# An attention-and-gated-MLP kernel with K and V of one head laid over all 128 partitions, some transposes moved to the DMA crossbar, and a new order list

## The chip, the cores and the metric

The kernel runs on one core of one Trainium2 chip. The metric is the device time of one execution in microseconds, the median of several runs. The engines are TensorE (PE, with its weight loads as PEld), VectorE (DVE), ScalarE (ACT), GpSimd (POOL) and SyncE (SP, which here only issues transfers).

## The reference

```python
def phi(x):                                        # x: [8, 8, 576, 64]
    proj = np.einsum('bhsd,df->bhsf', x, w_phi)    # 64 -> 128 features
    proj = proj - np.max(np.abs(proj), axis=-1, keepdims=True)
    return np.concatenate([np.exp(proj), np.exp(-proj)], axis=-1)
q_p, k_p = (phi(q), phi(k))
kv = np.einsum('bhsf,bhsd->bhfd', k_p, v)
z = np.sum(k_p, axis=2)
num = np.einsum('bhsf,bhfd->bhsd', q_p, kv)
den = np.einsum('bhsf,bhf->bhs', q_p, z)[..., None] + 1e-06
x = num / den                                      # then heads side by side: [8, 576, 512]
gate = sigmoid(sum over 5 taps k of conv_w[k] * x shifted down by 4 - k)
out = (gate * (x @ w_val)) @ w_out
```

There are 8 batches of 8 heads with 576 tokens of 64 numbers each. All inputs and the output are float32; the kernel multiplies in bf16.

## The kernel before, in words

**Tiling.** Two heads make a unit: `hp` is the pair, so units 0 to 31 are four per batch. A head's 576 tokens are 64 rows of 9 (`J`); token 9p + j lies on partition p in "plane" j. One head of the pair uses partitions 0 to 63, the other 64 to 127. Planes 0 to 7 of a unit are its main part; plane 8 of all four units of a batch is a "tail" unit (32 to 39).

**Steps of a unit**, each a function `op_...` and a token of the order list:

- `LD`: GpSimd issues the load of K, Q or V of a batch (of one or two units in batch 0), with the cast to bf16 in the transfer (L311). Each of K, Q, V has three buffers.
- `T` (L329, tails L325): TensorE transposes K and Q, eight 128x128 products into one PSUM bank; `C` copies the bank to the tile `T` in SBUF (L197 on VectorE or L195 on ScalarE). There are five such tiles.
- `PK`, `PA` (L341): projections of K and Q with tokens on partitions, into two banks each, as products on half the array's rows (64 of 128), in pairs. `MK`, `MQ` (L359): VectorE takes the maxima of absolute values.
- `K0`, `K1` (L384): ScalarE's two exponentials of K's projection, into `KT`. `E` (L378): exp of minus and plus the maximum, two small instructions per unit. `V` (L409, L413): GpSimd multiplies V by that, into `VT`, with a column for the sum z.
- `KV` (L427): TensorE sums KT x VT over the tokens, 36 half-array products per unit, the two heads in two banks; `KM` copies them to `KVSA`.
- `PQ` (L441): Q's projection with features on partitions; `SH` (L450): eight products subtract the maximum in PSUM; `X0`, `X1` (L384): the exponentials into `QT`.
- `N` (L492, tails L481): numerator and denominator; `XN` (L510, L512): reciprocal and product; `XP` transposes XN into `XT`, by the DMA crossbar from SP's queue (L531) for 28 units, on TensorE with a copy `XX` for the others.

**Steps of a batch.** `HL` copies the halo of four planes in `XT` (L197). `GF` (L571): the five conv taps as 80 products on 32x32 pieces of the array; `TH` (L595): tanh. `VA`, `VB` (L600): x @ w_val; `GV` (L616): gate. `OA`, `OB` (L629): @ w_out; `OE` (L638, L640): copy to SBUF; `ST`, `SL` (L650): store. `GT` (L673), `VT` (L684), `HT`, `GW`, `OT`, `OF`, `SU` do the same for plane 8, with 64x64 pieces for the taps.

**What sets the order.** Each engine takes its instructions strictly in the order of the string `ORDER`, a list of tokens: `PK.5@0,1` is the step PK of unit 5 into PSUM banks 0 and 1, `:D`, `:A`, `:P` name VectorE, ScalarE or GpSimd. PSUM has eight banks, all given out by the list. An instruction that waits holds up everything behind it on its engine, and the transfers behind it on its queue.

Of the kernel before, what the change touches and what calls it, by code (L numbers as in the profile page):

```python
# [20 lines left out]
HP = 4  # L21
J = 9
E1 = D + 1

# [3 lines left out]
LW.0 LC.0 CK.0:D LD.0 CQ.0:A LD.1 LD.2 LD.3 W.0:A LD.4 T.0@6 C.0:D LD.5 ND.0:D PK.0@4,5 PA.0@6,7 LD.6 K0.0  # L28
MQ.0 LD.7 K1.0 T.1@3 LD.8 PQ.0@0,1 MK.0 C.1:A SH.0 LD.9 X0.0 PK.1@2,3 PA.1@6,7 LD.10 MK.1 E.0 X1.0 V.0:P MQ.1
K1.1 TP.0@1 T.2@5 E.1 PQ.1@6,7 C.2:D K0.1 SH.1 LD.11 CW.0:D PK.2@4,5 X1.1 T.32@0 MK.2 LD.12 PA.2@2,3 X0.1  # L30
C.32:D MQ.2 E.2 K0.2 PK.32@6,7 LD.13 V.1:P MK.32 K1.2 PQ.2@2,3 T.3@0 SH.2 E.32 C.3:D K0.32 V.32:P X1.2
PA.3@0,1 MQ.32 PK.3@4,5 MQ.3 V.2:P K1.32 X0.2 PQ.32@6,7 SH.32 MK.3 KV.1@0,1 X0.32 KV.0@2,3 X1.32 DG.0:P KM.1:D
K1.3 N.1@6,7 PQ.3@0,1 K0.3 XN.1 SH.3 KM.0:D LW.1 XP.1 T.33@6 X1.3 N.0@2,3 C.33:D PK.33@6,7 X0.3 XN.0 KV.2@4,5
MK.33 T.4@1 MQ.33 E.33 T.5@0 KM.2:A C.4:D K0.33 N.2@2,3 K1.33 C.5:D T.6@1 E.3 T.7@5 XN.2 C.6:A V.3:P PK.4@6,7
C.7:D XP.2 PA.5@2,3 K1.4 MQ.5 PA.4@4,5 XP.0 PK.5@0,1 K0.4 CV.0:P MQ.4 PQ.5@2,3 SH.5 K1.5 MK.4 KV.3@4,5 X0.5
KM.3:D X1.5 PQ.4@6,7 MK.5 SH.4 E.4 X1.4 N.32@2 T.34@3 XN.32 N.3@4,5 C.34:D E.5 V.4:P X0.4 T.10@3 XN.3 XP.32@2
C.10:D XX.32:A PA.6@6,7 XP.3 PK.6@4,5 K0.5 MQ.6 T.9@3 V.33:P T.8@2 K0.6 C.9:D PQ.6@6,7 V.5:P K1.6 KV.4@0,1
C.8:D SH.6 KM.4:D MK.6 N.4@0,1 X1.6 LD.14 KV.5@2,3 X0.6 HL.0:D XN.4 GT.0@4,5 LD.15 KM.5:A VT.0 HT.0 E.6
N.5@0,1 V.6:P GF.0@2,3,6,7 XN.5 GW.0 XP.5 VA.0@0 TH.1 XP.4 VB.0 LD.16 PK.7@4,5 TH.0 KV.6@6,7 MK.7 CO.0:P
VA.3@1 KM.6:A VB.3 GV.0 K0.7 VA.1@7 GV.3 N.6@2,3 E.7 VA.2@6 K1.7 XN.6 VB.1 VB.2 XP.6 GV.1 PK.34@0,1 PA.7@2,3  # L40
GV.2 V.7:P K0.34 PQ.33@4,5 SH.33 MQ.7 OA.1@7 K1.34 OA.0@6 X0.33 OB.0 X1.33 MK.34 PQ.7@2,3 LD.17 PK.8@4,5 MQ.34
E.34 SH.7 OE.0:A MK.8 V.34:P KV.7@0,1 X0.7 OB.1 KM.7:D E.8 OA.2@6 X1.7 OE.1:D V.8:P PA.8@0,1 N.33@7 MQ.8 K0.8
N.7@2,3 OB.2 K1.8 XN.7 PQ.8@0,1 SH.8 XN.33 XP.7 PK.9@2,3 OE.2:D X0.8 XP.33@5 OA.3@7 XX.33:D MK.9 OB.3 X1.8
PA.9@4,5 T.11@6 OE.3:A MQ.9 KV.8@0,1 K0.9 T.35@7 KM.8:D E.9 PQ.9@4,5 C.35:D K1.9 SH.9 V.9:P C.11:D N.8@0,1
HL.1:D X1.9 PK.10@6,7 XN.8 GT.1@2,3 VT.1 MK.10 HT.1 X0.9 LD.18 KV.9@0,1 GW.1 KM.9:A LD.19 PA.10@4,5 K1.10
N.9@2,3 MQ.10 OT.0@0 K0.10 XN.9 PQ.10@4,5 E.10 SH.10 OF.0:D V.10:P XP.9 GF.1@2,3,6,7 X0.10 XP.8 X1.10 ST.1
VA.4@1 VA.7@0 TH.3 PK.11@4,5 VB.4 ST.0 MK.11 TH.2 VB.7 KV.10@6,7 GV.7 SU.0 VA.6@3 KM.10:A GV.4 K0.11 VB.6
N.10@6,7 GV.6 K1.11 VA.5@2 XN.10 VB.5 E.11 PK.35@0,1 GV.5 XP.10 PA.11@4,5 V.11:P K0.35 PQ.34@6,7 SH.34 MQ.11
T.12@3 K1.35 OA.4@2 X0.34 OB.4 MK.35 X1.34 PQ.11@4,5 C.12:A OE.4:D SH.11 MQ.35 KV.11@6,7 E.35 X1.11 V.35:P
PK.12@2,3 KM.11:D OA.5@1 MK.12 X0.11 OB.5 LD.20 PA.12@6,7 OE.5:A T.13@0 MQ.12 E.12 N.11@4,5 K1.12 V.12:P  # L50
# [53 lines left out]
def kernel(  # L104
# [24 lines left out]
    featq = pool("featq", 4)  # L129
    featt = pool("featt", 2)  # L130
    vtp = pool("vtp", 4)
    vttp = pool("vttp", 2)
    xnp = pool("xnp", 4)
    mlpp = pool("mlpp", 2)
    outp = pool("outp", 2)
# [15 lines left out]
    def main_tile(name, b):  # L151
        if (name, b) not in main:
            main[name, b] = loadp[name].tile([P, HP, J, D], BF16, name=name + "N")
# [611 lines left out]
```

## Time and profile before

| | |
|---|---|
| runs | 236.83, 240.39, 240.66 us; median 240.39 |
| profiled execution, from first to last instruction | 240.9 us |
| mean granted TensorE clock | 0.979 |
| instructions on PE, DVE, ACT, POOL | 4473, 285, 316, 141 |
| DMA traffic | 30.39 MB in 32982 packets |
| HBM | 30.48 MB read, 9.44 MB written |

The profile takes one execution. A row of its groups reads: line, engine, operation, output <- inputs, shapes, count, then total busy time in us and mean ns of one, then the idle time just before them and what ended it. A matmul's busy time holds its latency, so the distance from start to start in the timeline tells more than the mean. A stage's row gives the stretch and, for each engine, its busy time and number of instructions.

### The profile page before, as it was taken

Reading aid. Unit: us, or ns where it says so; the run is one execution under the profiler, and the core shown is the slowest. Engines: PE = TensorE matmul, PEld = TensorE weight load, DVE = VectorE, ACT = ScalarE, POOL = GpSimd, SP = SyncE. Lnnn points to the kernel's source line nnn. Section 1 sums busy time; section 2 is a strip of 40 time slices with the busy share of each in tenths; the row PEclk is TensorE's granted clock in tenths of the full one; section 3 lists DMA queues with packets and bytes.
Section 4 is the critical chain, followed back from the end, with each engine's and each line's share of the span. In section 5 each row is a group of like instructions: output and inputs, shape, how many; then the busy total and the mean of one; then the engine's idle time right before and its main releaser. Section 6 shows DMA issues by size and latency. Waiting matters only on the chain.

```text
span 240.9 us, 10034 instructions
## 1 busy us (share of the span) xinstructions
PE 208.8 (87%) x4473; PEld 140.6 (58%) x4500; DVE 180.9 (75%) x285; ACT 188.9 (78%) x316; POOL 109.3 (45%) x141
## 2 busy tenths in 40 slices
PE   1777997996998999679998999899995999999990
PEld 1455775853575566556665566666773666676540
DVE  2568599965999699479985899789985588897540
ACT  3688789963997999749988889999994799986531
POOL 8487939774525169135334335333543035542000
PEclk9999999997999999999999999999999799999997
DMA  6999972399936949993969693321559216000476
GB/s 147 280 257 217 209 115 47 41 187 109 143 35 104 249 135 164 201 194 104 179 131 123 94 150 69 69 71 25 112 101 218 88 26 112 3 3 3 129 225 177
DMA packets 32982, 30.39 MB, mean 126 GB/s; under 512 B 16677, under 2 KB 28837, under 8 KB 32938
## 3 DMA queue, kind: packets, MB, share of 16 engines
q0 software_dynamic: 12512, 13.86, 38.1%
q1 hardware_dynamic: 19882, 15.03, 29.5%
q10 hardware_dynamic: 544, 0.85, 1.2%
q8 instruction: 35, 0.57, 1.0%
q14 instruction: 9, 0.07, 0.1%
HBM read 30.48 MB, written 9.44 MB: 166 GB/s over the span
## 4 chain that ended last, share of the span: by engine, by line
PE 60%; DVE 21%; issue 6%; DMA 5%; ACT 5%; POOL 0%; ACTq 0%; DVEq 0%; POOLq 0%
PE PS L600 12%; PE PS L629 9%; PE PS L450 7%; PE PS L427 6%; PE PS L341 5%; PE PS L492 5%; DVE MQA L359 5%; DVE MKA L359 5%; PE PS L571 4%; PE PS L441 4%; PE PS L329 3%; DMA qN<-in_q_dram 3%; DVE T L197 3%; DVE XN L512 3%; ACT QT L384 2%
## 5 line engine op out<-in xcount | busy, mean ns | idle before, releaser
L409 POOL TENSOR_TENSOR VT<-vN,EA 128x1024 bf16<-128x1024 bf16 x32 | 60.9, 1904 | 90.4 <-issue 68.8
L384 ACT ACTIVATE QT<-PS 128x1024 bf16<-128x1024 f32 x64 | 63.2, 1028 | 12.5 <-PE PS L450 12.2
L384 ACT ACTIVATE KT<-PS 128x1024 bf16<-128x1024 f32 x64 | 63.1, 1027 | 2.2 <-DVE MKA L359 1.2
L359 DVE TENSOR_REDUCE MKA<-PS 128x8 f32<-128x1024 f32 (+1 forms) x40 | 44.3, 1112 | 16.3 <-PE PS L341 16.0
L359 DVE TENSOR_REDUCE MQA<-PS 128x8 bf16<-128x1024 f32 (+1 forms) x40 | 44.4, 1112 | 4.5 <-PE PS L341 4.2
L600 PE MATMUL PS<-XT,WVAL 128*128 128x512 bf16 x128 | 33.6, 389 | 2.0 <-issue 1.9
L629 PE MATMUL PS<-WOUT,GV 128*128 128x512 bf16 x105 | 30.4, 382 | 2.1 <-issue 1.6
L341 PE MATMUL PS<-W,T 64*128 64x128 bf16 x512 | 26.6, 232 | 1.9 <-DVE T L197 1.2
L450 PE MATMUL PS<-nident,MQA 128*128 128x128 bf16 x288 | 25.6, 235 | 1.5 <-issue 1.5
L427 PE MATMUL PS<-VT,KT 64*128 64x65 bf16 x1024 | 24.3, 196 | 2.6 <-issue 1.7
L616 DVE SCALAR_TENSOR_TENSOR GV<-GATE,PS 128x512 bf16<-128x512 bf16 x32 | 21.4, 683 | 5.7 <-PE PS L600 4.8
L427 PEld LDWEIGHTS <-KT 64*128 64x128 bf16 x1024 | 20.7, 98 | 6.7 <-issue 3.8
L450 PEld LDWEIGHTS <-MQA 128*128 128x128 bf16 x288 | 18.3, 105 | 10.1 <-issue 9.5
L341 PEld LDWEIGHTS <-T 64*128 64x128 bf16 x512 | 17.0, 100 | 11.5 <-issue 7.2
L512 DVE TENSOR_TENSOR XN<-PS,RCPA 128x512 bf16<-128x512 f32 x32 | 22.1, 691 | 1.1
L492 PE MATMUL PS<-KVSA,QT 128*128 128x65 bf16 x512 | 21.9, 196 | 1.0 <-DVE KVSA L197 0.5
L492 PEld LDWEIGHTS <-QT 128*128 128x128 bf16 x512 | 19.6, 99 | 5.5 <-DVE GVt L699 0.5
L197 DVE COPY T<-PS 128x1024 bf16<-128x1024 bf16 x27 | 18.0, 682 | 3.1 <-PE PS L329 3.0
L595 ACT ACTIVATE GATE<-PS 128x1024 bf16<-128x1024 f32 x16 | 16.0, 1028 | 5.4 <-PE PS L571 5.4
L600 PEld LDWEIGHTS <-WVAL 128*128 128x128 bf16 x128 | 10.9, 99 | 12.7 <-issue 4.0
L329 PE MATMUL PS<-ident_bf,kN 128*128 128x128 bf16 x128 | 13.3, 230 | 5.5 <-DVE kN L197 5.1
L441 PE MATMUL PS<-T,W 64*128 64x512 bf16 x64 | 13.5, 416 | 1.5 <-DVE MQA L359 1.0
(78 smaller groups left out, 293.8 us busy)
## 6 DMA issues: line engine op xcount, KB each, us to landing
out_dram<-OS SPq DMA_DIRECT2D x28, 256.0 KB, 4.2
kN<-in_k_dram POOLq DMA_DIRECT2D x7, 576.0 KB, 6.8
qN<-in_q_dram POOLq DMA_DIRECT2D x7, 576.0 KB, 9.8
vN<-in_v_dram POOLq DMA_DIRECT2D x7, 576.0 KB, 8.7
OS<-in_moe_w_val_dram SPq DMA_DIRECT2D x1, 1024.0 KB, 10.5
out_dram<-OSt SPq DMA_DIRECT2D x8, 128.0 KB, 2.4
OS<-in_moe_w_out_dram SPq DMA_DIRECT2D x8, 64.0 KB, 9.7
out_dram<-OS ACTq DMA_DIRECT2D x4, 128.0 KB, 2.7
```

The lines of the kernel that those rows point to most:

```text
L197: read(engines[eng].tensor_copy(dst, x), bank)
L341: nc.tensor.matmul(PS[:, bank[par], c0 + blk * P:c0 + (blk + 1) * P], u.T[r, i, blk, :], W2[r, :], start=True, stop=True,)
L359: read(nc.vector.tensor_reduce(dst[:, :, 0:n], banks(*bank)[:, :, c0:c0 + n * F].rearrange("p a (b f) -> p a b f", f=F), AX.X, ALU.max, ap ...
L384: read(nc.scalar.activation(dst, banks(*bank)[:, :, 0:n * P].rearrange("p r (x t) -> p r x t", t=dst.shape[-1]), AF.Exp, scale=1.0 if ft = ...
L409: e.tensor_tensor(u.VT[:, :, :, 0:D], x.unsqueeze(1).to_broadcast([P, 2, n, D]), w.unsqueeze(3).to_broadcast([P, 2, n, D]), ALU.mult,)
L427: nc.tensor.matmul(PS[:, bank[h2], ft * E1:(ft + 1) * E1], kt, vt, start=(j == 0), stop=(j == 8),)
L441: nc.tensor.matmul(PS[:, bank[par], 0:n], W2[r, :], u.T[r, 1, :, :].rearrange("p b t -> p (b t)"), start=True, stop=True,)
L450: nc.tensor.matmul(PS[:, u.PQ[par], blk * P:(blk + 1) * P], MQA[:, i, par, blk:blk + 1].to_broadcast([P, P]), nident[:, :], start=False, s ...
L492: nc.tensor.matmul(PS[:, bank[c // 2], x * E1:(x + 1) * E1], u.QT[:, ft, c, h2, :, :].rearrange("p j t -> p (j t)"), kv[:, h2, ft * E1:(ft ...
L512: read(nc.vector.tensor_tensor(u.XN[:, :, :, :], nv[:, :, :, 0:D], rc.unsqueeze(3).to_broadcast([P, 2, 4, D]), ALU.mult,), u.N)
L600: nc.tensor.matmul(PS[:, m.val[jt], :], WVAL[:, dt, jt * P:(jt + 1) * P], planes(xt(m.b), slice(0, P), dt, 4), start=(dt == 0), stop=(dt = ...
L629: nc.tensor.matmul(PS[:, bank, :], lhs(jt), WOUT[:, jt, :], start=(jt == 0), stop=(jt == 3))
```

## The change

- **One head on 128 partitions.** K and V of a head are split in two halves of its rows' planes: partitions 0 to 63 hold planes 0 to 4, partitions 64 to 127 planes 4 to 8 of the same head (`J + 1` planes a unit, plane 4 twice). Each load of K or V becomes two transfers, one for each half. Q stays as it was.
- **KV sums on the whole array.** The two halves of a head are summed in one product on 128 rows: 16 products of 65 columns per unit and 2 of 130 columns for the tail, all in one bank instead of two. The tail's V goes to a zero-padded tile `VTZ` in two parts of 64 partitions. `KVSA` has 16 places instead of 32.
- **Plane-8 taps on the whole array** (`GT`): 20 products with a 128x128 matrix `DIAGF` instead of 40 with 64x64 pieces.
- **Wide projections.** A token with `:W` projects with the zero-padded `W2Z` on the whole array: 4 units and 5 tails of PQ, 8 of PK and PA.
- **Split shifts.** `SH` becomes `SA` and `SB`, each half of the shift; with `:F` the step SA does the whole as before and SB nothing. In the list every SA has `:F`.
- **Crossbar.** `TK` and `TQ` transpose K and Q of units 16 to 31 by DMA from SP's queue, straight into the tile `T`; these units have no `T`, no `C` and no bank for them.
- **E for two units** in one pair of instructions.
- **Fillers.** 24 tokens `FL`: a product of zeros, 512 columns; 12 of them stand behind the last real product.
- **A new list**, with other banks, engines and places for most steps.

Core of the diff:

```diff
-            main[name, b] = loadp[name].tile([P, HP, J, D], BF16, name=name + "N")
+            main[name, b] = loadp[name].tile([P, HP, J if name == "q" else J + 1, D], BF16, name=name + "N")
...
+    def main_dma(eng, name, b, h0, h1, dst):
+        x = src[name][b, 2 * h0:2 * h1, :, :]
+        if name == "q":
+            eng.dma_start(
+                dst.rearrange("p a j d -> p a (j d)"), x.rearrange("(hp t) (p j) d -> (t p) hp (j d)", t=2, j=J),
+            )
+            return
+        x = x.rearrange("h (p j) d -> p h (j d)", j=J)
+        for r in range(2):
+            eng.dma_start(
+                dst[r * 64:(r + 1) * 64, :, :, :].rearrange("p a (t j) d -> p (a t) (j d)", t=2),
+                x[:, :, r * 4 * D:(r * 4 + 5) * D],
+            )
...
+    def op_FL(i, bank):
+        nc.tensor.matmul(PS[:, bank[0], :], zero[:, 0:P], zero[:, :], start=True, stop=True)
...
+    def crossbar(i, x, name):
+        u = units[i]
+        if not hasattr(u, "T"):
+            u.T = ktp.tile([P, 2, 4, P], BF16, name="T")
+        j = 0 if name == "q" else 1
+        nc.sync.dma_start_transpose(
+            u.T[:, x, :, :], main[name, u.b][:, u.hp, j:j + 8, :].rearrange("p j d -> p (j d)"),
+        )
...
+            if wide:
+                x, c = (i, blk) if u.tail else (blk // 2, blk % 2)
+                nc.tensor.matmul(
+                    PS[:, bank[x], c * 2 * F:(c + 1) * 2 * F], u.T[:, i, blk, :],
+                    W2Z[:, :, :].rearrange("p a f -> p (a f)"), start=True, stop=True,
+                )
+                continue
...
     def op_E(i):
-        n = 2 if units[i].tail else 4
+        x, n = (slice(i, i + 1), 2) if units[i].tail else (slice(i, i + 2), 4)
...
-            for j in range(J):
-                for h2 in range(2):
-                    r = slice(h2 * 64, h2 * 64 + 64)
...
-                    nc.tensor.matmul(
-                        PS[:, bank[h2], ft * E1:(ft + 1) * E1], kt, vt, start=(j == 0), stop=(j == 8),
-                    )
+            for j in range(8):
+                c = (2 * ft + j // 4) * E1
+                nc.tensor.matmul(
+                    PS[:, bank[0], c:c + E1], u.KT[:, ft, j // 2, j % 2, :], u.VT[:, ft, j, :],
+                    start=(ft == 0 and j == 0), stop=False, skip_group_check=True,
+                )
+        for ft in range(2):
+            nc.tensor.matmul(
+                PS[:, bank[0], 2 * ft * E1:2 * (ft + 1) * E1], t.KT[:, ft, u.hp // 2, u.hp % 2, :],
+                t.VT[:, ft, u.hp, :, :].rearrange("p h e -> p (h e)"),
+                start=False, stop=True, skip_group_check=True,
+            )
...
-                for r in range(2):
-                    for x in range(2):
-                        dt = 2 * x + s
-                        rows = slice(r * 64, r * 64 + 64)
-                        cols = slice((r ^ x) * 64, (r ^ x) * 64 + 64)
+                    nc.tensor.matmul(
+                        PS[:, bank[x], s * 64:s * 64 + 64], DIAGF[:, 2 * x + s, tap, :],
+                        XT[:, 2 * x + s, (8 + tap) * 64:(9 + tap) * 64],
+                        start=(tap == 0), stop=(tap == 4), skip_group_check=True,
+                    )
...
-LW.0 LC.0 CK.0:D LD.0 CQ.0:A LD.1 LD.2 LD.3 W.0:A LD.4 T.0@6 C.0:D LD.5 ND.0:D PK.0@4,5 PA.0@6,7 LD.6 K0.0
+LD.1 CK.0:A CQ.0:D FL.16@0 W.0:D LD.0 LD.7 LD.4 LC.0 T.0@0 C.0:D LD.6 LD.3 WB.0:D T.1@1 PK.0@2,3 K0.0 PA.0@4,5
```

How the instructions move, at three places.

On SP's queue, in the last third of the program, before (XN is a unit's attention result, XT its transposed place, OS and OSt are output tiles):

```order
L531 DMA_TRANSPOSE XT0_117<-XN_2950 128x4x128
L531 DMA_TRANSPOSE XT0_117<-XN_3201 128x4x128
L531 DMA_TRANSPOSE XT0_117<-XN_3310 128x4x128
L531 DMA_TRANSPOSE XT0_117<-XN_3483 128x4x128
L718 DMA out_0_dram<-OSt_3207 64x512 x2
```

and in the change (T is a unit's transposed K and Q, kN and qN the loaded K and Q):

```order
L758 DMA out_0_dram<-OS_2914 64x1024 x2
L371 DMA_TRANSPOSE T_3174<-kN_2471 128x4x128
L371 DMA_TRANSPOSE T_3242<-qN_2438 128x4x128
L371 DMA_TRANSPOSE T_3174<-qN_1977 128x4x128
L371 DMA_TRANSPOSE T_3424<-qN_1977 128x4x128
L371 DMA_TRANSPOSE T_3424<-kN_2471 128x4x128
L371 DMA_TRANSPOSE T_2968<-qN_1977 128x4x128
L371 DMA_TRANSPOSE T_3533<-qN_2438 128x4x128
L822 DMA out_0_dram<-OSt_3473 64x512 x2
L647 DMA_TRANSPOSE XT1_125<-XN_3523 128x4x128
L647 DMA_TRANSPOSE XT1_125<-XN_3576 128x4x128
```

The queue now carries 32 transposes of K and Q among its 28 of XN and the stores, in one order; the tile T_3174 gets its two halves at two places.

On ScalarE, near the middle, before (EA holds the weights for V, KT and QT the exponentials of K and Q, KTt and QTt those of a tail):

```order
L378 ACTIVATE EA_131<-MKA_129 128x2x4 x2
L384 ACTIVATE KT_2499<-PS_100 128x1024 x2
L693 ACTIVATE GATEt_2525<-PS_100 128x256
L384 ACTIVATE QT_2547<-PS_100 128x2x8x64 x2
L378 ACTIVATE EA_131<-MKA_129 128x2x4 x2
L384 ACTIVATE KT_2597<-PS_100 128x1024 x2
```

and in the change:

```order
L473 ACTIVATE KT_2429<-PS_97 128x2x4x128 x2
L746 ACTIVATE OS_2442<-PS_97 128x512 x2
L473 ACTIVATE KT_2469<-PS_97 128x2x4x128 x2
L457 ACTIVATE EA_137<-MKA_135 128x2x8 x2
L457 ACTIVATE EA_137<-MKA_135 128x4 x2
L746 ACTIVATE OS_2442<-PS_97 128x512
```

EA comes once for two units, behind the second one's K, where it came once for each.

On GpSimd, at the start, before (vN is the loaded V, VT the weighted V):

```order
L311 DMA qN<-in_q_dram 128x576
L311 DMA vN<-in_v_dram 128x2x576
L311 DMA kN<-in_k_dram 128x4x576
L311 DMA qN<-in_q_dram 128x4x576
L409 TENSOR_TENSOR VT<-vN,EA 128x16x64
```

and in the change (VTZ is the tail's weighted V, zero-padded):

```order
L162 DMA qN<-in_q_dram 128x576
L168 DMA kN<-in_k_dram 64x2x320 x2
L162 DMA qN<-in_q_dram 128x576 x2
L168 DMA kN<-in_k_dram 64x2x320 x4
L168 DMA vN<-in_v_dram 64x2x320 x4
L168 DMA vN<-in_v_dram 64x4x320 x2
L168 DMA kN<-in_k_dram 64x8x320 x2
L162 DMA qN<-in_q_dram 128x4x576
L168 DMA vN<-in_v_dram 64x8x320 x2
L168 DMA kN<-in_k_dram 64x8x320 x2
L494 TENSOR_TENSOR VTZ_115<-vN,EA 64x8x64
```

Q comes first, V of batch 0 last, and 22 transfers stand ahead of the first product of V where 11 stood.

365 lines of the change are left out of this document (213 added, 152 removed).

## The prediction

> **What bounds the kernel now.** I read the engines' busy time first, then the chain of work that ended last.
>
> ```profile
> PE 208.8 (87%) x4473; PEld 140.6 (58%) x4500; DVE 180.9 (75%) x285; ACT 188.9 (78%) x316; POOL 109.3 (45%) x141
> ...
> PE 60%; DVE 21%; issue 6%; DMA 5%; ACT 5%; POOL 0%; ACTq 0%; DVEq 0%; POOLq 0%
> ```
>
> No engine is full. The chain runs mostly through TensorE, and a fifth of it through VectorE's maxima and copies. Next come the stages (columns: stretch, then busy us and instructions of PE, PEld, DVE, ACT, POOL, then granted clock, DMA share, GB/s).
>
> ```profile
> 0.00:20.00 20.00, 11.01 (x112) 7.53 (x113) 10.18 (x16) 12.46 (x20) 13.92 (x24) 1.00 0.99 229
> 20.00:220.00 200.00, 182.77 (x4126) 124.96 (x4150) 162.83 (x254) 169.35 (x286) 95.36 (x117) 0.98 0.69 113
> 220.00:241.00 21.00, 15.07 (x237) 8.13 (x237) 7.91 (x16) 7.11 (x12) 0.00 (x0) 0.92 0.53 152
> ```
>
> ```profile
> 40.00:60.00 20.00, 17.43 (x436) 12.04 (x430) 14.26 (x26) 13.39 (x23) 14.16 (x15) 0.92 0.88 100
> ...
> 160.00:180.00 20.00, 19.38 (x499) 13.80 (x495) 18.09 (x30) 18.82 (x33) 8.29 (x9) 1.00 0.36 72
> 180.00:200.00 20.00, 17.37 (x302) 11.02 (x303) 13.93 (x20) 14.80 (x28) 4.72 (x5) 0.91 0.49 103
> ```
>
> The 200 us between 20 and 220 decide. In its best stage (160 to 180) three engines stand at 90% to 97% together; in weak ones (40 to 60, 180 to 200) all three sag together. Each unit is passed from TensorE to VectorE or ScalarE and back through eight PSUM banks, and nobody is far ahead. The table of waits says the same from the other side:
>
> ```profile
> POOL VT L409 <- issue: 68.8, 19, 10.0
> ...
> DVE MKA L359 <- PE PS L341: 16.0, 14, 2.5
> ACT QT L384 <- PE PS L450: 12.2, 16, 2.5
> ```
>
> VectorE and ScalarE wait for TensorE's projections and shifts. GpSimd waits a lot and is in nobody's way. So I take the middle to shrink with the work of the three engines, not of one.
>
> **The change part by part. TensorE.** Rows of its timeline (start, us, instructions in the row):
>
> ```profile
> 165.21 0.39 PE L329 MATMUL PS<-ident_bf,kN 128*128 128x128 bf16 x4
> ...
> 165.66 0.59 PE L629 MATMUL PS<-WOUT,GV 128*128 128x512 bf16 x2
> ...
> 166.51 0.62 PE L450 MATMUL PS<-nident,MQA 128*128 128x128 bf16 x8
> ...
> 167.06 0.43 PE L427 MATMUL PS<-VT,KT 64*128 64x65 bf16 x16
> ```
>
> The first row opens a unit's eight transposes, four of K and four of Q; up to the next product of whole-array shape they take 0.45 us (165.21 to 165.66). Sixteen units lose them: -7.2. Eight shifts of the same size take 0.55 (166.51 to 167.06) where a product on half the array's rows follows (64*128 in the form). So I read a change of the array's shape as 0.10 us. The order of TensorE's instructions has 232 such changes before and 164 now: 68 x 0.10 = -6.8.
>
> ```profile
> 133.21 0.39 PE L441 MATMUL PS<-T,W 64*128 64x512 bf16 x2
> 133.53 0.62 PE L450 MATMUL PS<-nident,MQA 128*128 128x128 bf16 x8
> 134.09 0.40 PE L341 MATMUL PS<-W,T 64*128 64x128 bf16 x8
> 134.32 0.42 PE L427 MATMUL PS<-VT,KT 64*128 64x65 bf16 x16
> ...
> 134.99 0.30 PE L325 MATMUL PS<-ident_bf,kN 128*64 128x128 bf16 x4
> ```
>
> ```profile
> 136.80 0.51 PE PS L492 x16
> ```
>
> ```profile
> 127.67 0.51 PE L673 MATMUL PS<-XT,DIAG 64*64 64x64 bf16 x40
> 128.11 0.64 PE L684 MATMUL PS<-XT,WVAL 128*128 128x64 bf16 x16
> 128.68 0.43 PE L427 MATMUL PS<-VT,KT 64*128 64x65 bf16 x16
> ```
>
> A KV sum is 36 half-array products, two at a time, in 0.67 us less up to 0.10 for the shape change: 0.57. Now it is 16 whole-array products of 65 columns, at 0.51 by the N products of that size, and two of 130 at 0.055 (a 128-column transpose): 0.62. So halving the count buys nothing: +0.04 x 32 = +1.3. Plane-8 taps took 0.44 - 0.10 for 40 and become 20 whole-array products at 0.57/16: 0.71, +0.3 x 8 = +2.6 at most. The wide projections lose their pairing: PQ is 0.32 - 0.10 = 0.22 for two half-array products and 0.43 whole (4 units, 5 tails of half size), PK or PA 0.23 against 0.43 (8 times): +3.0. Sum for TensorE: -7.1 of 182.8, 3.9%. The 24 fillers (FL, 512 columns, 0.22 each) count 0, since half stand behind the last product and the others where the list had nothing to run; if none were covered, +5.2.
>
> **ScalarE and VectorE** (count | busy, mean ns):
>
> ```profile
> L197 DVE COPY T<-PS 128x1024 bf16<-128x1024 bf16 x27 | 18.0, 682 | 3.1 <-PE PS L329 3.0
> L378 ACT ACTIVATE EA<-MKA 128x8 f32<-128x8 f32 x64 | 10.0, 213 | 2.1 <-DVE MKA L359 2.1
> L195 ACT ACTIVATE KVSA<-PS 128x260 bf16<-128x260 f32 x19 | 7.4, 387 | 1.4 <-PE PS L427 1.2
> L197 DVE CAST KVSA<-PS 128x260 bf16<-128x260 f32 x13 | 5.5, 424 | 3.1 <-PE PS L427 3.1
> L195 ACT ACTIVATE T<-PS 128x1024 bf16<-128x1024 bf16 x5 | 5.2, 1034 | 0.7 <-PE PS L329 0.6
> L197 DVE COPY XT<-XT 128x1008 bf16<-128x1008 bf16 x7 | 4.8, 686 | 1.4 <-DMA XT<-XN 1.3
> ```
>
> ScalarE: EA for two units in one pair of instructions, 64 to 32, half of 10.0: -5.0; copies of T 5 to 1: -4.1; KVSA 19 to 13: -2.3; smaller forms together -0.3: -11.7, 6.9% of 169.35. VectorE: T 27 to 15, -8.2; KVSA 13 to 19, +2.5; the halo copies XT 7 to 2, -3.4; the rest +0.4: -8.7, 5.3% of 162.83. The new memsets (about 3 us) run before the first K arrives, when VectorE is idle.
>
> The mean of 3.9, 6.9 and 5.3% is 5.4%: -10.7 of the 200 us. By TensorE alone it is -7.8, by ScalarE alone -13.8; these two are the term's bounds.
>
> **GpSimd** gains work:
>
> ```profile
> L409 POOL TENSOR_TENSOR VTt<-vN,EA 128x512 bf16<-128x512 bf16 x8 | 8.4, 1044 | 11.2 <-ACT EA L378 11.2
> L311 POOL DMA_DIRECT2D kN<-in_k_dram x10 | 7.3, 734 | 2.7 <-DMA qN<-in_q_dram 2.3 <-issue 0.3
> L197 POOL COPY XT<-XT 128x1008 bf16<-128x1008 bf16 x1 | 1.0, 1024 | 2.7 <-DVE MQA L359 2.7
> ```
>
> Twenty more load issues (+15 at the same price each), eight more tail products (+8.4, with their casts +10), five more halo copies (+5): about 140 us of 231. Its own waits (68.8 us before V in the table above) cover this: 0. EA now comes for two units at once, so the first unit's V starts up to a unit later (200/32 = 6 us); the list puts KV behind that. Without this cover V is late, then KV, KM and N, and behind N on TensorE everything else.
>
> **DMA.** K and V lie now as two overlapping halves, two transfers instead of one; 32 crossbar transposes (K and Q of units 16 to 31) join SP's queue.
>
> ```profile
> DMA packets 32982, 30.39 MB, mean 126 GB/s; under 512 B 16677, under 2 KB 28837, under 8 KB 32938
> ...
> q0 software_dynamic: 12512, 13.86, 38.1%
> ...
> XT<-XN SPq DMA_TRANSPOSE x28, 4.3
> ```
>
> ```profile
> 192.00:198.00 6.00, 5.95 (x96) 3.57 (x96) 5.86 (x9) 5.51 (x12) 2.10 (x2) 1.00 0.13 26
> ```
>
> Loads take 38.1% of 240.9: 91.8 us of all 16 engines, K and V 61. The halves carry 10/9 of the bytes (+6.8 at least) in twice the packets (+61 if a packet's price stays). The stretch 192 to 198 holds one crossbar transpose and no load: 0.13 x 6 = 0.8 us, 32 of them +25. From 0.99 x 20 + 0.69 x 200 + about 11 = 169 busy us the queues go to between 201 and 255. The transposes move 128 KB in 0.8 us, 160 GB/s; the loads 13.86 MB in 91.8, 151 GB/s. Only the transposes can make up most of the 16677 packets under 512 B, and they are no slower by the byte than the loads' larger ones. So price goes with bytes, and I take the low end with some room: about 205 of 231. It stays hidden, if barely: 0, with the upper end a rival.
>
> The Trainium skill's Advanced Engine Details and Errata (X-Bar Transpose (TRN2)) gives transposes 350 to 400 GB/s; by that 128 KB are an estimated 0.35 us and the 32 cost 11, and by that the queues would end at 190 us and the rival below on DMA would keep half its chance. The row's 0.8 us disagrees, and the row decides.
>
> **Start.** The order puts both transposes of units 0 and 1 ahead of PK.0, which ran at 6.92; unit 1's second load landed at 9.44:
>
> ```profile
> 2.34 7.10 DMA qN<-in_q_dram
> ```
>
> ```profile
> 6.92 1.03 PE L341 MATMUL PS<-W,T 64*128 64x128 bf16 x16 [0.79 <-DVE T L197]
> ```
>
> So PK.0 slips by 3.1 us to about 10.0 (9.44, T.1's 0.45, and a shape change). Unit 1 needed that landing before as well, and loses nothing. Between 0 and +3.1 I take the middle, +1.5: ScalarE idles until K0.0, but the second unit is ready right behind it.
>
> The Trainium skill's DMA: Bandwidth & Descriptors (Rules for kernel authors) speaks against the halves: two transfers to disjoint partition halves serialise. With the 2.0 us per transfer that its fit gives, the start would be an estimated +3.5 and the sum 2 us more. No run here shows it yet.
>
> Sum: 240.9 - 10.7 + 1.5 = 231.7 in the profiled execution, which stands 0.5 above the median of the runs (240.39): **231.2**.
>
> **Rivals.** *The crossbar takes the gain.* PK of units 16 to 31 now waits for a transfer instead of a copy, and everything behind PK on TensorE waits with it; ScalarE and VectorE run dry one exponential later. Between TK.28 and PK.28 the list has GT.5, GF.5, VT.5 and a filler:
>
> ```profile
> 77.70 1.28 PE PS L571 x80
> ```
>
> 1.28 + 0.71 + 0.57 + 0.22 = 2.8 us on TensorE, and a transpose lands in 4.3 at the median. TK.29 and TK.31 stand as close. SP also takes all of them in order behind XP and the stores. For it: the queues get fuller, and landing slower with them. Against: most TK and TQ stand more than a unit ahead, and all loads but one are issued before TK.31. If a unit lost half a microsecond on average: 231.2 + 16 x 0.5 = 239. *DMA becomes the bound.* If a packet's price does not fall with its size, the queues need 255 us, and the kernel ends near that: 252, slower than before. It decides from a total of about 231: the halves may then cost 231 - 169 - 25 = 37 us more than K and V do now, 98 against 61, that is 1.6 times the time for 1.1 times the bytes. Against: the transposes' rate by the byte above. *The stages close up.* T needs no bank in 16 units and KV one bank instead of two. If all stages reach the density of 160 to 180, TensorE's 182.8 - 7.1 = 175.7 us take 175.7 / 19.38 x 20 = 181 instead of 200: 240.9 - 19 + 1.5 - 0.5 = 223. For it: weak stages were waits, not work. Against: the list before had the same aim.
>
> **How the numbers follow.** Forecast (226 to 235.6) 0.46; closed stages 0.20; crossbar takes the gain 0.22; DMA bound 0.12. Two per cent (4.8 us) is about what a measurement of this kernel tells from no change, so faster is 0.66, same 0.22, slower 0.12. The likeliest case's own range is 226 to 236; the range that reaches to the others is 221 to 243.
>
> **What would show it.** PE's transposes x128, T copies 15 on VectorE and 1 on ScalarE, EA 48; ScalarE's busy time near 177, VectorE's near 173; N products against KV products at the same 32 ns; PK waiting for a DMA of T under 5 us in all; a DMA share near 0.9 until 150. Wrong if long waits of L404 on T's transposes appear, if K's landing doubles, or if busy sums fall as said and the span does not.

## The result: 252.6 us, slower than before

The changed kernel takes 252.6 us (median of four executions, 249.04 to 260.12) beside 240.5 us for the kernel before on the same chip: ratio 1.0479, 95% interval 1.0363 to 1.0595. Times are medians of all executions; the ratios, here and below, leave out executions over 1.5% above the shortest of the same kernel (here 254.85 and 260.12), and the profile of the kernel before, with its span of 240.9 us, is of such a longer one. The forecast was 231.2 us, range 221 to 243, so both the time and the sign were wrong.

The profiled execution took 249.04 us. Its page, for the changed kernel: busy time, then the DMA packets and queues, then the chain that ended last.

```profile
span 247.2 us, 8486 instructions
...
PE 204.2 (83%) x3665; PEld 137.9 (56%) x3692; DVE 175.7 (71%) x282; ACT 179.1 (72%) x272; POOL 136.1 (55%) x190
...
DMA packets 58912, 35.55 MB, mean 144 GB/s; under 512 B 34421, under 2 KB 54901, under 8 KB 58874
...
q1 hardware_dynamic: 37434, 19.26, 44.2%
q0 software_dynamic: 20896, 14.90, 43.6%
...
PE 52%; DMA 17%; ACT 14%; DVE 9%; issue 3%; POOL 2%; SPq 1%; DVEq 0%; POOLq 0%; ACTq 0%
```

The three engines did lose work: TensorE 4.6 us, VectorE 5.2, ScalarE 9.8. The span grew by 6.3 us all the same, and by the ratio the loss is 11.4. DMA is 17% of the chain that ended last, where it was 5%, and the packets grew from 32982 to 58912. The stages show where (columns as in the prediction's table; first two of the kernel before, then the changed kernel):

```profile
100.00:120.00 20.00, 17.25 (x383) 11.50 (x370) 15.75 (x25) 15.48 (x27) 7.21 (x7) 1.00 0.92 163
120.00:140.00 20.00, 18.67 (x441) 12.44 (x443) 15.76 (x26) 17.38 (x30) 9.33 (x12) 1.00 0.83 124
```

```profile
80.00:100.00 20.00, 19.16 (x310) 12.27 (x311) 17.11 (x29) 19.57 (x31) 13.40 (x16) 1.00 1.19 157
100.00:120.00 20.00, 17.89 (x397) 12.93 (x401) 18.09 (x29) 16.22 (x29) 7.54 (x9) 1.00 1.13 150
120.00:140.00 20.00, 12.27 (x238) 8.06 (x237) 7.79 (x12) 9.89 (x15) 12.78 (x15) 0.83 1.11 192
140.00:160.00 20.00, 19.28 (x367) 12.46 (x366) 17.55 (x28) 18.63 (x31) 12.71 (x16) 1.00 1.16 138
```

One stage is a hole: from 120 to 140 us all three engines run dry together while the DMA share stands at 1.11 (the column adds up the packets' times, and can pass 1), against 0.83 before the change. The granted clock is 0.83 in it, too, and 1.00 in the stages on both sides. TensorE's table of waits names what ends them (us in total, times, longest):

```profile
PE PS L777 <- DMA XT<-XN: 7.5, 1, 7.5
PE PS L364 <- ACT kN L220: 6.8, 1, 6.8
PE PS L687 <- DVE XT L222: 3.1, 1, 3.1
...
PE PS L404 <- DMA T<-kN: 1.8, 1, 1.8
PE PS L397 <- DMA T<-kN: 1.8, 1, 1.8
```

The long one, at L777 (GT.3), is not a wait for the new transfers. It is a wait for an old one, the transpose of XN into XT, which the new ones stand in front of. SP's timeline shows the queue at that place, and the chain shows what it cost:

```profile
109.75 2.47 SPq L371 DMA_TRANSPOSE T<-kN  x1
112.26 1.96 SPq L371 DMA_TRANSPOSE T<-qN  x1
114.31 8.24 SPq L647 DMA_TRANSPOSE XT<-XN  x3
```

```profile
120.08 9.24 DMA XT<-XN
129.37 1.22 PE PS L777 x20
```

SP needs 2 to 2.5 us to issue one transfer there and 8.24 us for three; the last of them is issued at 120.08 and its wait on the chain lasts 9.24 us. By the median, the new transfers landed 7.0 and 7.5 us after their issue:

```profile
T<-qN SPq DMA_TRANSPOSE x16, 7.0
T<-kN SPq DMA_TRANSPOSE x16, 7.5
```

### The profile page after: what moved, and what is told of

Read it like the earlier page. It is cut to its first block, busy times and chain, and to the rows that moved or that the text cites. A ratio compares the mean times of both kernels' runs of the same rounds, so it can differ in the third digit from the quotient of the medians.

```text
span 247.2 us, 8486 instructions
## 1 busy us (share of the span) xinstructions
PE 204.2 (83%) x3665; PEld 137.9 (56%) x3692; DVE 175.7 (71%) x282; ACT 179.1 (72%) x272; POOL 136.1 (55%) x190
## 4 chain that ended last, share of the span: by engine, by line
PE 52%; DMA 17%; ACT 14%; DVE 9%; issue 3%; POOL 2%; SPq 1%; DVEq 0%; POOLq 0%; ACTq 0%
PE PS L737 11%; DMA XT<-XN 10%; PE PS L708 9%; ACT KT L473 5%; ACT QT L464 5%; PE PS L608 4%; PE PS L404 4%; DMA kN<-in_k_dram 4%; PE PS L516 4%; PE PS L562 4%; DMA T<-kN 3%; PE PS L687 3%; PE PS L539 3%; ACT GATE L703 2%; DVE MKA L439 2%
## 5 line engine op out<-in xcount | busy, mean ns | idle before, releaser
L708 PE MATMUL PS<-XT,WVAL 128*128 128x512 bf16 x128 | 37.6, 397 | 0.1
L724 DVE SCALAR_TENSOR_TENSOR GV<-GATE,PS 128x512 bf16<-128x512 bf16 x32 | 21.3, 681 | 17.1 <-PE PS L708 11.2
L494 POOL TENSOR_TENSOR VTZ<-vN,EA 64x512 bf16<-64x512 bf16 x16 | 16.7, 1046 | 19.9 <-ACT EA L457 19.4
L404 PE MATMUL PS<-W,T 64*128 64x128 bf16 x448 | 21.4, 224 | 3.7 <-DMA T<-kN 1.8
L562 PE MATMUL PS<-nident,MQA 128*128 128x128 bf16 x288 | 23.2, 222 | 0.4 <-DVE MQA L439 0.4
L516 PE MATMUL PS<-VT,KT 128*128 128x65 bf16 x512 | 22.4, 197 | 0.8 <-POOL VT L507 0.7
L516 PEld LDWEIGHTS <-KT 128*128 128x128 bf16 x512 | 20.4, 100 | 4.1 <-issue 1.0
L222 POOL COPY XT<-XT 128x1008 bf16<-128x1008 bf16 x6 | 6.2, 1028 | 27.7 <-DVE XT L222 13.9
L404 PEld LDWEIGHTS <-T 64*128 64x128 bf16 x448 | 14.4, 97 | 12.1 <-issue 6.3
L746 ACT ACTIVATE OS<-PS 128x512 f32<-128x512 f32 x21 | 12.3, 600 | 9.6 <-PE PS L737 9.6
L168 POOL DMA_DIRECT2D vN<-in_v_dram x20 | 13.5, 682 | 5.1 <-DMA qN<-in_q_dram 3.8
```

Source lines behind the costliest of these rows:

```text
L404: nc.tensor.matmul(PS[:, bank[par], c0 + blk * P:c0 + (blk + 1) * P], u.T[r, i, blk, :], W2[r, :], start=True, stop=True,)
L516: nc.tensor.matmul(PS[:, bank[0], c:c + E1], u.KT[:, ft, j // 2, j % 2, :], u.VT[:, ft, j, :], start=(ft == 0 and j == 0), stop=False, ski ...
L562: nc.tensor.matmul(PS[:, u.PQ[par], blk * P:(blk + 1) * P], MQA[:, i, blk, par:par + 1].to_broadcast([P, P]), nident[:, :], start=False, s ...
L708: nc.tensor.matmul(PS[:, m.val[jt], :], WVAL[:, dt, jt * P:(jt + 1) * P], planes(xt(m.b), slice(0, P), dt, 4), start=(dt == 0), stop=(dt = ...
L724: read(nc.vector.scalar_tensor_tensor(out=m.GV[:, jt, :, :, :].rearrange("p n i t -> p (n i t)"), in0=m.GATE[jt // 2][:, jt % 2, :], scala ...
```

## The experiments

All ratios are to the kernel before, run beside it on the same chip, with 95% intervals. My first theory was that the crossbar's transfers load the DMA engines until XN lands late; the rival was that the new list or the new products cost.

**Taking the crossbar out of the change, and leaving only its load in.** a_no_crossbar puts the TensorE transposes back into the new list; b_crossbar_unused also issues the 32 transfers, into buffers nobody reads.

```diff
-TK.16 ... TQ.16          (a and b, units 16 to 31)
+T.16@2 ... C.16:D        (T.16 26 steps ahead of PK.16)
+YK.16 ... YQ.16          (b alone, where TK and TQ stood)
```

> The changed kernel with the 32 crossbar transposes of K and Q taken out again: units 16 to 31 get their eight TensorE transposes and one copy out of PSUM back (11 copies on VectorE, 5 on ScalarE), some 20 steps of the list ahead of their use; split loads, whole-array KV sums, plane-8 taps, split shifts and the rest of the list stay. Theory (the crossbar's transfers fill the 16 DMA engines, and the transposes of XN and the transfers of K and Q land late, so that TensorE waits): DMA busy falls from about 220 us by 25 to 32, the median landing of XT<-XN goes back to about 3 us everywhere, the 7.5 us stall ahead of GT.3 goes, and although TensorE gets 7 us of work back the time is 236 to 241. Rival (the new list, the taps and the sums are what costs): nothing is gained and TensorE's 7 us come on top, 250 to 257.

> The kernel without crossbar transposes of K and Q (a_no_crossbar), but the same 32 crossbar transfers are still issued at their old places on SP, into buffers that nobody reads. Nothing waits for them. Theory (load on the shared DMA engines and on SP's queue, which makes the XN transposes late): the time goes back to 247 to 254, with XT<-XN landing 8 to 14 us after issue in the loaded stretches. Rival (what costs is that PK and PQ wait for their own T): the time stays within 2 us of a_no_crossbar, 236 to 242.

Measured: a 257.2 us, 1.0789 (1.0729 to 1.0849); b 271.1 us, 1.1361 (1.1278 to 1.1444). So b is some 13.6 us above a by the ratios: the transfers cost that much though no product reads what they bring, as the theory has it. But a did not come down to 241, it went up. Part of that is my own: I put 16 units' transposes and copies into a list that was made without them, and TensorE's short waits for T stand at many lines of it (1.8, 1.4, 1.2 us and less). So a does not tell the rival apart, and I took the kernel before and its list as the base from here.

**The loads' halves and the start, undone in the changed kernel.**

```diff
+        if eng is nc.gpsimd:                                  (c_whole_loads)
+            eng.dma_start(dst[:, :, 1:, :]..., x.rearrange("(hp t) (p j) d -> (t p) hp (j d)", ...))
+            return
-    for name, eng in (("k", nc.sync), ("q", nc.scalar)):      (d_start)
+    for name, eng in (("k", (nc.sync, nc.scalar)), ("q", nc.scalar)):
-LD.1 CK.0:A CQ.0:D
+LD.1 CK.0:D CQ.0:A
```

> The changed kernel with the K and V loads after the first as one transfer of nine planes each instead of two of five (crossbar stays). K and V then lie one head below the other as before the change, so the KV sums mix the two heads and the output is another; every instruction but the loads keeps its shape. Theory: the loads' 16 us of engine time come off (107 to 91), some transposes land earlier, and the time falls by a part of what the crossbar costs: 243 to 247. Rival (loads run far ahead and their size does not matter): 248 to 251.

> The changed kernel with its start mended: the two halves of the first K go out on SP's and ScalarE's queues in place of one behind the other on SP, and the first K is converted by VectorE and the first Q by ScalarE, so that ScalarE's table load does not sit behind the wait for K. Theory: the first exponential starts 2 to 3 us sooner (11.0 to about 8.5), and since nothing else is mended it is partly lost again at the next late transfer: 246 to 249. Rival (the start is on the path all the way): the whole 3 us, 245 to 247; rival (the DMA engines set the pace): nothing, 248 to 251.

Measured: c 250.2 us, 1.0421 (1.0332 to 1.0511); d 250.5 us, 1.0513 (1.0460 to 1.0566). c is at best a little under the changed kernel's 1.0479, within the intervals. d gained nothing, by its third expectation, but not for its reason: TensorE's timeline of d_start shows the start being mended and given back.

```profile
5.67 0.61 PE L360 MATMUL PS<-ident_bf,kN 128*128 128x128 bf16 x4 [3.87 <-DVE kN L218]
6.66 0.61 PE L360 MATMUL PS<-ident_bf,qN 128*128 128x128 bf16 x4 [0.38 <-ACT qN L216]
9.98 0.58 PE L360 MATMUL PS<-ident_bf,kN 128*128 128x128 bf16 x4 [2.72 <-DMA kN<-in_k_dram]
```

T.0 now starts at 5.67 us (8.56 in the changed kernel). T.1, which the list puts ahead of PK.0, waits for the second unit's K, and that landed at 9.8 us instead of 7.1. The first exponential comes at 11.57 us, against 11.03.

**One part at a time in the kernel before.** e_before_crossbar has the crossbar and nothing else of the change; f_before_crossbar_unused only its load; g_before_split only the halves; h_old_list is the converse, the changed program by the list of before, without the crossbar, and so without wide projections, fillers and E for two units.

```diff
-T.16@1 ... C.16:D                        (e; units 16 to 31)
+TK.16 TQ.16                              (e; some 85 steps ahead of PK.16)
+YK.16 YQ.16                              (f; the same places, T and C kept)
-        nc.gpsimd.dma_start(main_tile(name, b)[:, h0:h1, :, :]..., main_src(name, b, h0, h1))
+        for r in range(2):                (g)
+            nc.gpsimd.dma_start(dst[r * 64:(r + 1) * 64, ...], x[:, :, r * 4 * D:(r * 4 + 5) * D])
-SH.0                                      (h: the order of before with these words changed, and other banks for the tails' T)
+SA.0:F
-KV.1@0,1
+KV.1@0
```

> The kernel before with one part of the change alone: units 16 to 31 lose their eight TensorE transposes and the copy out of PSUM, and get the two crossbar transposes instead, issued on SP 80 steps of the list (about three units) ahead of PK; loads, KV sums, taps and the rest of the list as before. The run with unused crossbar transfers cost 13.9 us over the one without, so theory (the transfers' load on the DMA engines costs about 14 us, the work taken off TensorE, VectorE and ScalarE gives 8 to 11 back): 241 to 246. Rival (the crossbar is worth what the prediction said, and the new list is what costs): 228 to 234.

> The kernel before, unchanged in all its work (only the first K and Q are staged in GV's buffers, for room), plus the same 32 crossbar transfers at the same places as in e_before_crossbar, into buffers that nobody reads. Theory (load on the DMA engines, whatever the list): 250 to 254. Rival (the 13.9 us are a matter of the new list, in which every transfer is tight; with the loads of before the engines have room): 238 to 242.

> The kernel before with another part of the change alone: each K and V load is two transfers of five planes instead of one of nine (11% more bytes, twice the packets). The planes are then read as if they lay as before, so K and V rows go to other tokens and heads and the output is another; every instruction but the loads keeps its shape. Theory (engine time of DMA costs like the crossbar's, 16 us against 28 for 14 us): 8 us, 243 to 248. Rival (loads run well ahead of their use, only the crossbar transfers matter): 237 to 240.

> The changed kernel's program (split loads, whole-array KV sums, plane-8 taps, shifts whole, the start) run by the list of before: TensorE transposes for all units, no crossbar of K and Q, no wide projections, no warm-up products, the exponentials of the maxima unit by unit. Theory (the new list is a large part of the loss, since without the crossbar the new list takes 257): 237 to 245. Rival (the new pieces themselves cost, whatever the list): 248 to 258.

Measured: e 243.5 us, 1.0276 (1.0165 to 1.0387); f 250.9 us, 1.0604 (1.0515 to 1.0693); g 240.4 us, 1.0165 (1.0104 to 1.0226); h 244.5 us, 1.0366 (1.0282 to 1.0450). The crossbar alone makes the kernel before slower, its bare load by twice as much (with a late start in it, see below), and the rest of the program is slower without any crossbar. e, f and h came out in the ranges of my theory, g between its two. So there are two losses, not one. f shows the same hole as the changed kernel, although all its arithmetic and its list are those of before:

```profile
100.00:120.00 20.00, 18.73 (x329) 11.30 (x326) 17.54 (x27) 17.00 (x29) 8.39 (x10) 1.00 1.21 179
120.00:140.00 20.00, 12.40 (x247) 7.04 (x246) 6.70 (x11) 7.70 (x14) 6.34 (x7) 0.74 1.06 114
140.00:160.00 20.00, 19.42 (x414) 13.00 (x413) 17.86 (x27) 18.40 (x33) 7.67 (x8) 1.00 0.83 130
```

```profile
117.38 7.21 DMA XT<-XN
```

Four unused transfers stand on SP from 108.8 to 117.3; the XN transpose behind them is issued at 117.38 and is on the chain for 7.21 us. Another 3.4 us of this hole are a stall of TensorE that the last section treats. So the wait in it is made by load and queue order, not by a wait for T.

**Where the transfers are, and a clean price.** In f and g the first Q went out behind half of w_phi and landed at 7.6 and 6.8 us instead of 4.7, a side effect of my staging; k and l repeat them without it. i and j split e in two.

```diff
-T.24@3 ... C.24:A     +TK.24 TQ.24     (i: units 24 to 31; j: units 16 to 23)
-        y = dump.tile([P, 4, P], BF16, name="Y")                    (k, against f)
+        y = spare[i % 2 + (2 if name == "q" else 0)]                # halves of first K's and first Q's tiles
-        first[name] = mlpp.tile([P, 4, 4, 2, 64], BF16, name="GV")  (l, against g: for K alone)
+        first["q"] = const.tile([P, 1, J * D], FP32, name="qF")
```

> The kernel before with crossbar transposes of K and Q for units 24 to 31 alone (eight units, 16 transfers, 80 steps of the list ahead of PK), TensorE transposes for the rest. In e_before_crossbar these 16 were issued after 149 us, when the loads of all batches were through, and landed in about 2.7 us; the 16 of units 16 to 23 were issued from 90 to 142 us, among the loads of batches 4 to 7, and landed in about 8. Theory (a transfer costs only where it meets the loads): the work taken off the engines is kept and nothing is paid, 232 to 236. Rival (each of the 32 transfers costs alike, wherever it is): half of the 6 us of e_before_crossbar, 239 to 242.

> The same with crossbar transposes for units 16 to 23 alone, the transfers that meet the loads. Theory: it pays the whole price of e_before_crossbar and keeps half of the gain, 243 to 248. Rival (each transfer alike): 239 to 242.

> f_before_crossbar_unused once more, with the unused transfers written over the staging tiles of the first K and Q, which are free by then, so that the start is that of the kernel before. (In f_before_crossbar_unused the first Q went out behind half of w_phi on ScalarE's queue, landed at 7.6 us instead of 4.7, and the first exponential started at 10.4 instead of 7.6.) Theory (2 to 3 us of the 14 were the start, the rest the transfers): 246 to 249. Rival (the start is absorbed, all of it is the transfers): 250 to 252.

> g_before_split once more (loads of K and V split, the planes read as before, so the output is another), with the first Q staged as before the change, so that its load keeps its place ahead of w_phi. Theory (2 of the 4 us were the start, the split loads themselves cost little): 238 to 240. Rival (the loads cost 4 us): 240 to 242.

Measured: i 237.6 us, 1.0036 (0.9954 to 1.0118); j 242.3 us, 1.0226 (1.0116 to 1.0336); k 245.2 to 250.7 us, its ratio, 1.037, resting on the shortest execution alone and without an interval; l 241.8 us, 1.0233 (1.0131 to 1.0335). i and j add up to e (0.4 + 2.3 against 2.8%), and nearly all the loss sits in the half that meets the loads, so the rival of equal prices falls. But my theory's 232 to 236 for i was missed too: it did not become faster. By that k is 8.8 us above the kernel before, where f was 14.3; one execution is little, so the bare price of the 32 transfers lies between these two, and how much of the difference is the start stays open. The hole is in k as well, smaller:

```profile
120.00:140.00 20.00, 15.11 (x339) 9.45 (x336) 11.01 (x19) 11.98 (x19) 7.14 (x8) 0.91 0.95 135
```

l did not come down from g. The halves cost 4 to 5.5 us by themselves.

**What is still hidden in i, in h, and in XN.** m issues the 16 late transfers unused; n takes the halves out of h; s gives 12 XN transposes of the changed kernel to TensorE; u is h with the crossbar, that is, the changed program by the old list.

```diff
+YK.24 YQ.24                                   (m; units 24 to 31, T and C kept)
+        if eng is nc.gpsimd: ... return       (n; h with c's loads)
-XP.12
+XP.12@0 ... XX.12:D                           (s; units 8 to 19, D and A in turn)
-T.16@1 ... C.16:D     +TK.16 TQ.16            (u; h with e's words)
```

> The kernel before, all its work unchanged, plus the 16 crossbar transfers of units 24 to 31 alone into the free staging tiles (nobody reads them), issued after about 149 us. Theory (without loads beside it a transfer is free, and the work that i_crossbar_late took off was worth nothing): 236 to 239. Rival (the transfers cost 3 to 4 us, and i_crossbar_late earned as much): 240 to 242.

> h_old_list (the changed program by the list of before, without crossbar of K and Q) with the K and V loads after the first as one transfer each; K and V then lie as before the change, so the KV sums mix the heads and the output is another. Theory (split loads are 2 to 4 us of the 8.7, as by themselves): 239 to 242. Rival (the split is all of it): 236 to 238. Rival (none of it): 243 to 246.

> The changed kernel with the transposes of XN of units 8 to 19 (batches 2 to 4, the ones issued among loads and K, Q transfers) done by TensorE and copied by VectorE and ScalarE in turn, in place of the crossbar on SP; all else as changed. Adds about 12 x 0.4 us to TensorE and 12 x 0.7 us to the two others, takes 12 transfers out of SP's queue. Theory (late XN transposes are what TensorE waits for, the hole from 121 to 136 us closes): GF.3 starts at 126 to 130 instead of 135 and the time falls to 240 to 247. Rival (they are only one of several late transfers; K and Q are late as well): 248 to 254.

> The changed program with the crossbar for units 16 to 31, by the list of before (transfers 80 steps ahead of PK, no wide projections, no warm-up products). If the two prices add (3.7% for the program without crossbar, 2.8% for the crossbar in the kernel before): 250 to 254, and the new list has gained nothing over the old (252.6 with it). Rival (the new list is the loss): 240 to 246. Rival (the new list saves some, loads and transfers together are worse than their sum): 255 to 262.

Measured: m 239.8 us, 1.0147 (1.0032 to 1.0263); n 242.7 us, 1.0285 (1.0203 to 1.0366); s 249.9 us, 1.0579 (1.0477 to 1.0682); u 253.6 us, 1.0745 (1.0646 to 1.0844). m against i, by the middle values: the late transfers cost 3.5 us, and the work that they replace is worth 2.6; the two intervals overlap. u: the prices nearly add (3.7 and 2.8%, measured 7.5%, 6.5 to 8.4), and the new list, with its wide projections, fillers and E for two units, is not a loss but takes some 2.6% off, 1.0479 against 1.0745. n: the halves are only a part of h (0.8% by the middle values; the two intervals overlap). And s went against my theory: XN alone is not what matters. Its waits:

```profile
PE PS L401 <- DMA T<-kN: 4.7, 1, 4.7
PE PS L684 <- DVE XT L219: 4.2, 1, 4.2
```

The hole at 120 closed (18.55 us of TensorE in that stage) and the gate of batch 3 was 3.0 us earlier, 133.8 instead of 136.8; at the next batch nothing was left of it (159.8 and 159.9), since K's own transposes were late next (the 4.7 us above). s also put 3.3 us of work on TensorE, 2.9 on VectorE and 3.2 on ScalarE, so it does not say what XN's lateness alone costs.

**The taps, and GpSimd's share.** p is the kernel before with the plane-8 taps of the change alone; r takes the doubled tail pieces of V off GpSimd in h.

```diff
-                            PS[cols, bank[x], s * 64:s * 64 + 64], DIAG2[rows, dt, tap, :],   (p; 40 per batch)
-                            XT[rows, dt, (8 + tap) * 64:(9 + tap) * 64],
+                        PS[:, bank[x], s * 64:s * 64 + 64], DIAGF[:, 2 * x + s, tap, :],      (20 per batch)
+                        XT[:, 2 * x + s, (8 + tap) * 64:(9 + tap) * 64],
-            for h2 in range(2):                                       (r; tail V)
-                r = slice(h2 * 64, h2 * 64 + 64)
-                e.tensor_tensor(u.VT[r, :, :, h2, 0:D], ...)
+            e.tensor_tensor(u.VT[:, :, :, i % 2, 0:D], ...)
```

> The kernel before with the changed plane-8 taps alone: 20 products on the whole array per batch in place of 40 on quarters of it (the first K is staged in GV's buffer for room; the start is that of before). The prediction priced them at 2.6 us of TensorE. Theory (they are a part of the 6.7 us of n_old_list_whole_loads): 239 to 241. Rival (covered by waits of other engines): 236 to 238.

> h_old_list with the tail's V on GpSimd as one piece of 128 partitions instead of two of 64 (10 us of GpSimd less; the values of plane 8 go to one head, so the output is another). Theory (GpSimd, 19.4 us busy of the 20 from 20 to 40 us in h_old_list, is late there and TensorE waits): 2 to 4 us off, 240 to 243. Rival (its work is covered, as the prediction had it): 243.5 to 246.

Measured: p **231.9 us**, 0.9840 (0.9785 to 0.9894), from ten executions; r 242.3 us, 1.0300 (1.0128 to 1.0471). r is not told apart from h. p is faster than both kernels, by neither expectation. On TensorE the new taps are not cheaper (0.76 us per batch, from the first product to the end of the last, against 0.51); what went is idle time of TensorE for which the profile shows no releaser ("issue"). First the kernel before, then i_crossbar_late, which has the old taps too, then p:

```profile
PE PS L684 <- issue: 2.5, 1, 2.5
PE PS L600 <- issue: 1.9, 1, 1.9
PE PS L427 <- issue: 1.7, 2, 0.9
PE PS L629 <- issue: 1.6, 10, 0.2
PE PS L450 <- issue: 1.5, 1, 1.5
```

```profile
PE PS L438 <- issue: 3.7, 3, 3.1
PE PS L461 <- issue: 2.0, 1, 2.0
...
PE PS L611 <- issue: 0.8, 1, 0.8
```

```profile
PE PS L632 <- issue: 1.6, 10, 0.2
...
PE PS L495 <- issue: 0.8, 1, 0.8
...
PE PS L430 <- issue: 0.7, 1, 0.7
```

Counting single stalls of 0.5 us and more, the five of before sum to 7.6 us, those of i to 5.9 and the two of p to 1.5; the ten short ones at the products with w_out are alike in before and p. All nine traces with the old taps by the old list (before, e, f, g, i, j, k, l, m) have 5.8 to 8.7 us of them, those with the new taps by that list (p, h, n, r, u) 0.7 to 2.3.

## Why the prediction was wrong, point by point

- **The work taken off was sized roughly right; its worth is not settled.** Busy sums fell by 4.6 (TensorE), 9.8 (ScalarE) and 5.2 us (VectorE), against 7.1, 11.7 and 8.7 less about 3 of memsets. GpSimd rose by 26.8 (said: 30). The transposes' own part of the mean was 3.9, 2.4 and 5.0%, so 3.8% or 7.6 us. e is 6.5 us over before; with the same transfers and the work kept it was 8.8 (k) to 14.3 (f), so the work paid between 2 and 8.
- **The failed step is "It stays hidden, if barely: 0".** The sum it rested on was off by little: 89.7% of 247.2 = 222 us against "about 205". Loads went from 91.8 to 107.8 (+16, nearer the low end of +6.8 to +61, so price does go with bytes); the other hardware queue from 71 to 109, which is 1.2 us per crossbar transfer instead of 0.8. But to compare a total with the span was the mistake. In the stages from 80 to 160 the share stands at 1.1 to 1.2, transfers land late there, and the queues carry transposes that TensorE needs within a few microseconds. Price, with nobody reading them: 9 to 14 us for the 32 transfers (k and f), and 4 to 5.5 for the halves (g, l), where the prediction had 0.
- **"The crossbar takes the gain" (239) had the queue right and the victim wrong.** It had PK wait for T; that cost 3.6 us in the two rows above. XN and XT cost 10.6 there, since SP takes them in order behind the new transfers, as the rival's side remark said. The size, 239, was too small as well.
- **"DMA becomes the bound" (252) hit the number, but by luck, not by its cause.** Packets did not keep their price, and the total was 222 of a span of 247, not 255.
- **Start: +3.4 instead of +1.5.** The first exponential came at 11.03 us, not 7.58. PK.0 did not wait for T.1's load but for the first K: its halves landed at 4.0 and 6.4 us, one behind the other on SP, and ScalarE's table load came behind that wait:

```profile
6.47 1.28 ACT L220 ACT_TABLE_LOAD   x1 [6.47 <-DMA GV<-in_k_dram]
```

In the kernel before that load ran at 1.78 us, in idle time. The Trainium skill's DMA: Bandwidth & Descriptors (Rules for kernel authors), which has transfers to the two partition halves serialise, agrees with the 2.4 us between the halves on one queue; less so in d_start, where on two queues they landed at 4.9 and 4.0. How much of the 3.4 us is in the end is not settled: d moved it, it did not remove it.
- **Plane-8 taps: +2.6 said, 3.8 us gained (p).** Only the array's time was priced. By that the reckoning was right in sign (0.76 against 0.51 us, 2.0 in all); the 160 products and as many weight loads fewer in TensorE's stream were not priced at all.
- **The rest of the program stays partly open.** h is 3.7% slower with the taps in it, so its other parts cost some 5.3%, 12.5 us, if the taps are worth the same there as in p: halves 4 to 5.5 by themselves (2 inside it, n against h), the start about 2 (first exponential 9.4 against 7.6). Some 5 to 8 us are not assigned. h's TensorE waits 5.5 us for the copies of the tail's transposes (2.5, 1.7 and 1.3 in three rows), and GpSimd is busy 19.35 of the 20 us from 20 to 40; whether either is the cause was only read off, and r could not show it. Against p, with the same taps and nearly the same list, h is 5.1 us behind at the first plane-8 taps (49.8 against 44.7), 7.3 at the second and 11.2 at the last: some two thirds of the loss fall into the first 75 us.
- **What would show it wrong** was named, and one point came: busy sums fell as said and the span did not. K's landing went from 6.8 to 9.0 us, not to the double, though each transfer was half as large; and the DMA share, said to be near 0.9 until 150, stood at 1.1 to 1.2 from 80 on.

So the 4.8% come about like this: taps -1.6 and the other new pieces +5.3 (h, +3.7 together), the crossbar another 3.8 on top of h (u; 2.8 in e), and the new list -2.6, which is what lies between u and the changed kernel. These ratios were taken at different times, each with an interval of about 1% to either side, so the parts are rough.

## What to carry to other kernels

A transfer is hidden only if the stage that it falls into has room and if nothing urgent stands behind it in its queue; compare the DMA share stage by stage, and list what else that queue carries, before counting it as nothing. Issue a suspected transfer into a buffer that nobody reads: that gives its price without any wait of its own, in one experiment; see to it that the room for the buffer moves nothing else, as it moved the start in f. And price a change of products by the instructions it takes out of the stream as well as by the array's time.

## What the runs showed of the hardware that was not expected

**TensorE stops at fixed places of its instruction stream.** The stalls that end in "issue" come at one place modulo 256 when TensorE's recorded instructions (weight loads, products and a few control ones) are counted. In f_before_crossbar_unused, whose trace has all 4500 products beside 4500 weight loads, all of those over 0.7 us:

```
start us   stall us   instruction   modulo 256
 53.8       0.83       1730          194
103.2       1.27       3777          193
134.2       3.37       4803          195
194.0       3.21       7106          194
```

e has three such (1730, 3777, 6850: 194, 193, 194). Where products are missing from the record the count falls behind: 194, then 185, 185, 183 and 174 in the kernel before, which lacks 27. The timeline of the kernel before shows one, in the middle of 16 like products:

```profile
183.10 0.28 PE L684 MATMUL PS<-XT,WVAL 128*128 128x64 bf16 x4
185.84 0.52 PE L684 MATMUL PS<-XT,WVAL 128*128 128x64 bf16 x12 [2.47 <-issue]
```

A DMA queue of its own brings the instructions:

```profile
q8 instruction: 35, 0.57, 1.0%
```

35 packets of 16 KB for 9011 recorded instructions of TensorE in f make about 256 instructions of 64 bytes each; the changed kernel has 29 packets for 7368. In every kept trace each such stall of 0.7 us or more ends 1.2 to 1.7 us behind the end of one of these packets. So these are waits for the next block of instructions. The Trainium skill's Runtime: NRT & Kernel Launch (Instruction fetch mechanics) states the 16 KiB block of 256; it calls the cost of passing one mostly hidden, and here single ones cost 0.8 to 3.4 us (f). Most blocks come in time. Why some don't stays open: the stall at 185.84 begins 0.8 us behind the start of the last of 40 plane-8 products, which with their 40 weight loads are started in 0.32 us, and in p, with 20 of them, it is gone; but the one at 103.2 in f has no such burst in the 2 us before it, and a shorter stream also shifts where the blocks end. The stalls that went (5.9 us in i, 1.5 in p) less the 2.0 us of array time make 2.4 of p's 3.8; that they are its cause was not tried by itself.

**A hole costs more than its length.** In the holes the granted clock was lower as well: 0.83 in the changed kernel's, 0.74 in f's, 1.00 in the stages on both sides. The first products behind the changed kernel's hole were slower as well: the 20 plane-8 taps at 129.37 took 1.22 us on the chain, those at 106.06 0.58:

```profile
106.06 0.58 PE PS L777 x20
```

**A crossbar transfer is not free where few loads move.** In m, with one load left to go, those of K landed in 2.9 us and those of Q in 2.6 at the median, 2.4 at best; SP took 1.2 to 2.2 us to issue one, and the 16, read by nobody, cost 1.5% (0.3 to 2.6). Among the loads, in the changed kernel, issuing one took SP up to 3.7 us.
